# A planner's due times replaced by a written list of 1348 instructions: linear attention with a Hyena gate on one core

## The chip, the cores and the metric

The kernel runs on one core of a Trainium2 chip. The metric is the device time of one execution in microseconds (us); for a kernel it is the median over its runs. A profiled execution has an own time and a span, from its first to its last instruction; the span is a little shorter.

## The reference

Two layers follow each other. Batch is 8, heads 8, sequence S = 576, head width 64; 128 random features; model width 512.

```python
# attention with positive random features (per batch and head)
scale = 1 / sqrt(sqrt(64))
def phi(x):                                # x: q*scale or k*scale
    h = x @ omega.T - sum(x*x)/2
    return exp(h - max(h)) / sqrt(128)     # max over the features
kv  = phi(k).T @ v                         # 128 x 64
z   = sum over s of phi(k)
x   = (phi(q) @ kv) / (phi(q) @ z + 1e-6)  # 576 x 64; heads side by side: 576 x 512

# gated long convolution (per batch)
x1, x2, x3 = split(x @ w_proj, 3)          # 576 x 512 each
y   = x1 * irfft(rfft(x2) * rfft(filter)) * x3
out = y @ w_out
```

## The kernel before

**The attention.** The sequence of a batch is cut into a main part of 512 rows and a left part of 64, and the left parts of two batches are worked on as one tile of 128 rows. For each batch, keys are transposed (by TensorE through the one-bank PSUM tile "t", or from batch 5 on by a transposing DMA of SyncE), multiplied with omega into the two-bank tile "a2" (64 contraction rows), and put through ScalarE's exponential into ek (`key_features`). VectorE finds the largest feature of each row, whose reciprocal scales the values (`weigh_values`, giving vc). Queries go the same way into eqt. The sums kv come out of eight groups of matmuls; the rows of the output are divided by their denominators on VectorE (`normalise`) and turned back into xt. Loads are DMAs that GpSimd issues: k and v in one DMA of 512 KB for a batch, q from batch 2 on in four pieces of 128 KB, each left part in two halves of 64 KB. GpSimd issues in order, so a load whose buffer is not free stands ahead of all later loads.

**The convolution.** With S = 3 x 192, the transform is three transforms of length 192 over folded inputs, done as matmuls with tables of sines that the kernel makes at its start (`make_residues`, `sines`, `tables`). For each pair of batches: `fold` combines the three thirds of xt into xf, `project2` multiplies it by w_proj into x2, `forward` transforms and multiplies by the filter's spectrum, `gates` makes x1 * x3 (x13; of the left rows x13l), then come the inverse and the product with w_out. These use the PSUM tiles "h", one bank each, three of them in turn. The filter itself is folded and transformed once (`fold_filter`, `filter_transform`).

**What sets the order of issue.** The kernel's body isn't issued as it is written. `nc` is a `Plan`: every call on an engine is recorded as an `Op` with its number n, the tiles it reads and writes, and the stage and batch that `at` set; neighbouring matmuls into one tile are joined into one `Op`. 1348 are recorded: 396 of TensorE (PE), 475 of VectorE (DVE), 306 of ScalarE (ACT), 81 of GpSimd (POOL), 90 of SyncE (SP). Then `issue` emits them in the order that `order` returns. All instructions of the body so have line 405 in the profile, the line in `issue`; one tells them apart by the names of their tiles.

Before, `order` gives each operation a due time: the latest one at which its users could still be on time, worked back from the end of its batch (`PERIOD` and `STRETCH`), shifted by tables of numbers by stage, batch and engine (`LEAD`, `SHIFT`, `LEAN`). `simulate` then runs the program with modelled durations (`_cost`) and on each engine takes, of the operations that could start within 120 ns of the first, the one that is due first. It also hands out buffers in the order of its own program for each kind of tile and stage. The emitted instructions wait, as ever, for their data and for the buffer's earlier readers: a tile is given a slot of its pool when the first instruction that uses it is issued, so the order of issue also settles which earlier tile's readers a new tile waits for.

**The operations that are spoken of below**, by their number n:

| n | engine | what |
|---|---|---|
| 41 | DVE | factors for the residues (`make_residues`) |
| 224, 225 | PE, DVE | transposes of half of keys 2, and their copy into kt |
| 130, 131 | PE, ACT | turning back a quarter of the output rows of batch 0, and its copy into xt |
| 127 | PE | output rows of batch 0 (`a2` from kv and eqt) |
| 179 | ACT | last exponential of queries 1 |
| 600 | PE | first product of `fold` 0 (xf with w_proj, a bank h) |
| 248, 236 | PE | transposes of queries 2; of the left keys of batches 2 and 3 |
| 354, 417 | POOL | loads of keys 5, of keys 6 (512 KB each) |
| 145, 146 | POOL | two of the four pieces of queries 2 |
| 212 | POOL | one half of the left keys of batches 2 and 3 |
| 642 | SP | one of the moves of the filter's spectrum into hqs |
| 736, 435, 438 | DVE | the gate of the left rows, x13l, of the first pair; two steps of weighing values 5 |
| 823 | PE | a product of `fold` 3 (bank h) |
| 900, 949 | PE | a product of `gates` 3; one of the inverse of batch 3 |
| 809, 812 | DVE, PE | the fold of batch 2; the first product on it |
| 724, 697, 710, 828 | DVE | gate of batch 1, left spectrum, spectrum of batch 1, fold of left rows |
| 372 | PE | transposes of the left keys of batches 4 and 5 |
| 687, 267 | ACT | a copy of `forward` 0 (xs), the copy of kv of batch 2 |
| 367 | DVE | a copy of keys 4 into kt |

Of the kernel before, what the change touches and what calls it, by code (L numbers as in the profile page):

```python
# [24 lines left out]
PERIOD, STRETCH, STAY = 136.732, 16.038, 101.39  # L25
LEAD = {
    "cross keys": 0.92, "cross out": 7.64, "cross queries": -0.74, "filter": 4.65, "fold": -48.94,
    "forward": 107.85, "gates": -40.51, "inverse": 17.39, "keys": -0.75, "left keys": -52.95,
    "left out": -1.12, "left queries": -14.15, "load filter": 50.17, "load k": 55.36,
    "load kl": -1.11, "load q": -0.71, "load ql": 8.56, "load v": 0.49, "load vl": 1.73,  # L30
    "load w0": 1.61, "load w1": 5.28, "load w2": 1.64, "out": -42.88, "queries": 96.24,
    "residues": 1.41, "rest": 14.42, "sines": 0.5, "start": -189.65, "sums": -10.66,
    "tables": 0.2, "turn out": -3.18, "turn queries": 16.85, "values": -5.78, "zeros": 9.94,
}

SHIFT = {
    ("fold", 0): 48.94, ("fold", 1): 188.96, ("fold", 2): 50.05, ("fold", 7): 48.3,
    ("forward", 0): -112.16, ("forward", 1): -114.87, ("forward", 2): -107.32,
    ("forward", 6): -108.25, ("gates", 0): 16.24, ("gates", 1): 40.13, ("gates", 2): 50.94,
    ("gates", 6): 38.24, ("left keys", 2): 53.69, ("left keys", 6): 49.69, ("load k", 2): -56.64,  # L40
    ("load q", 0): -1.89, ("load ql", 0): -33.49, ("load v", 0): 2.07, ("load vl", 2): -6.7,
    ("queries", 1): -97.56, ("queries", 2): -131.03, ("queries", 6): -98.12,
    ("queries", 7): -93.75, ("rest", 1): 207.08, ("rest", 7): -14.42, ("turn out", 1): -12.03,
    ("turn out", 2): -153.32, ("turn queries", 1): -15.77, ("turn queries", 2): -16.64,
    ("values", 1): 546.29, ("values", 2): -24.51,
}
LEAN = {
    ("forward", "DVE"): 35.53, ("forward", "PE"): -40.96, ("gates", "DVE"): -10.03,
    ("gates", "PE"): 146.99, ("keys", "ACT"): -14.86, ("left queries", "ACT"): -47.8,
    ("queries", "ACT"): 5.49, ("queries", "PE"): 33.51, ("rest", "ACT"): -8.58,  # L50
    ("rest", "DVE"): -16.93,
}
# [33 lines left out]
class Op:  # L86
    __slots__ = (
        "eng", "calls", "reads", "writes", "due", "n", "busy", "lat", "deps", "users",
        "tiles", "start", "end", "name", "dma", "table", "where", "rows", "base",
    )  # L90

    def __init__(self, eng, due, n, name, where):
        self.eng, self.due, self.n, self.name, self.where = eng, due, n, name, where
        self.calls, self.reads, self.writes = [], [], []
        self.busy = self.lat = 0.0
        self.deps, self.users = {}, []
        self.tiles = set()
        self.dma = self.table = None
        self.rows = 128
# [13 lines left out]
class Plan:  # L113
# [4 lines left out]
    HOP = {"PE": 55.0, "DVE": 37.0, "ACT": 37.0, "POOL": 60.0, "SP": 60.0}  # L118

    def __init__(self, nc, tc):  # L120
        self.nc, self.tc = nc, tc
        self.ops, self.tile_of, self.slots = [], {}, {}
        self.where = "start", 0
        self.tensor = Proxy(self, "PE", nc.tensor)
        self.vector = Proxy(self, "DVE", nc.vector)
        self.scalar = Proxy(self, "ACT", nc.scalar)
        self.gpsimd = Proxy(self, "POOL", nc.gpsimd)
        self.sync = Proxy(self, "SP", nc.sync)
        self.allow_low_precision = nc.allow_low_precision
# [4 lines left out]
    def _new(self, eng, name):  # L134
        stage, b = self.where
        more = LEAD.get(stage, 0.0) + SHIFT.get((stage, b), 0.0) + LEAN.get((stage, eng), 0.0)
        op = Op(eng, more, len(self.ops), name, self.where)
        self.ops.append(op)
        return op

    def tile(self, pool, shape, dtype, name, bufs=1):
        t = pool.tile(shape, dtype, name=name, bufs=bufs)
        key = t.name if hasattr(t, "name") else t[:].tensor.name
        self.slots[pool.name, name] = bufs
        line = self.where[0]
        self.tile_of[key] = ((pool.name, name), "residues" if line == "load filter" else line)
        return t
# [7 lines left out]
    def record(self, eng, real, name, args, kw):  # L155
# [16 lines left out]
        if join:  # L172
            op = last
        else:
            op = self._new(eng, f"{name} {outs[0].tensor.name}")
            op.rows = ins[0].ap[0][1] if eng == "PE" else 128
# [5 lines left out]
        self._cost(op, eng, name, outs, ins)  # L182
        if name == "activation":
            op.table = {AF.Exp: "exp", AF.Sin: "sin"}.get(kw["func"])
        return op

    def opaque(self, eng, call, out, busy):
# [3 lines left out]
        op.busy = op.lat = busy  # L191

    @staticmethod
    def _free(ap):
        n = 1
        for _, c in ap.ap[1:]:
            n *= c
        return n

    def _cost(self, op, eng, name, outs, ins):  # L200
        out = outs[0]
        n = self._free(out)
        if name == "dma_start_transpose":
            op.busy, op.lat = 2000.0, 2200.0
            op.dma = ("HW", self._free(out) * 128 * 2 / 240.0)
            return
        if name == "dma_start":
            a = out if out.space != bass.MemoryType.DRAM else ins[0]
            run = a.ap[-1][1] * SIZE[a.dtype]
            rows = a.ap[0][1] * self._free(a) // a.ap[-1][1]  # L210
            if eng == "POOL":
                op.busy, op.lat = (880.0 if rows > 600 else 720.0), 3300.0
                op.dma = ("SW", rows * max(run, 166) / 198.0)
            elif out.space != bass.MemoryType.DRAM and ins[0].space == bass.MemoryType.DRAM:
                op.busy, op.lat = 580.0, 2300.0
                op.dma = ("HL", rows * run / 330.0)
            else:
                op.busy, op.lat = 580.0, 2000.0
                op.dma = ("HW", rows * run / 180.0 / (1 if out.space == bass.MemoryType.DRAM else 4))
            return  # L220
        half = all(SIZE[a.dtype] == 2 for a in (out, *ins))
        sbuf = all(a.space != bass.MemoryType.PSUM for a in (out, *ins))
        if eng == "PE":
            m = n / (4.8 if ins[0].ap[0][1] == 64 else 2.4) + 2.5
            op.lat = op.busy + n / 2.4 + 166.0
            op.busy += m
            return
        if eng == "DVE":
            if name == "memset":
                busy = n * SIZE[out.dtype] / 4.8 + 5.0  # L230
            elif name == "reciprocal":
                busy = 5.8 * n + 78.0
            elif name == "tensor_tensor":
                busy = n / (1.92 if half and sbuf else 0.96) + 68.0
            elif name == "scalar_tensor_tensor":
                busy = n / 0.96 + 130.0
            elif name in ("tensor_copy", "tensor_scalar", "tensor_scalar_mul"):
                rate = (4 if sbuf else 2) if half else (2 if sbuf else 1)
                if name != "tensor_copy" and not sbuf:
                    rate = 1  # L240
                busy = n / (0.96 * rate) + (68.0 if half else 100.0)
            elif name == "reduce_max":
                busy = self._free(ins[0]) / 0.96 + 60.0
            else:
                busy = n / 0.96 + 68.0
            op.busy, op.lat = busy, busy + 82.0
        elif eng == "ACT":
            busy = n * 0.8333 + (52.0 if not sbuf else 190.0)
            op.busy, op.lat = busy, busy + 107.0
        else:  # L250
            op.busy = op.lat = n / 1.2 + 100.0

    def order(self):
        last = {}
        for op in self.ops:
# [6 lines left out]
            for key, kind in ((op.reads, 0), (op.writes, 1)):  # L262
                for t, r in key:
                    last[t].append((op, kind, r))
                    if t in self.tile_of:
                        op.tiles.add(t)
        for op in self.ops:
            for o in op.deps.values():
                o.users.append(op)
        for op in reversed(self.ops):  # L270
            lat = op.lat + (op.dma[1] if op.dma else 0.0) + 50.0
            last = min((u.base for u in op.users), default=op.where[1] * PERIOD)
            op.base = last - STRETCH * lat / 1000.0
        for op in self.ops:
            op.due += op.base
            if op.eng == "PE":
                for u in op.users:
# [4 lines left out]
    def simulate(self):  # L282
# [8 lines left out]
        for op in ops:  # L291
            for t in op.tiles:
                left[t] = left.get(t, 0) + 1
# [1257 lines left out]
```

## Time and profile before

| | |
|---|---|
| runs | 266.75, 267.43, 267.69 us; median 267.43 |
| profiled execution, own time | 266.88 us |
| its span | 264.8 us |
| TensorE clock granted | 1.00 of full speed throughout |
| busy: PE, DVE, ACT, POOL | 239.7, 213.4, 195.2, 61.3 us |
| DMA | 36.31 MB, mean 137 GB/s |

Busy time is the time in which an engine had an instruction under way; loads of TensorE's weights (PEld) overlap its matmuls. "Idle before" is the time between the end of one instruction and the start of the next on the same engine, and the releaser is what the trace shows as ended last before it. An idle stretch of an engine costs something only where the end of the program hangs on that engine.

### The profile page before, as it was taken

How to read it: one execution, taken by the hardware profiler on the slowest of the kernel's cores; microseconds unless marked ns; L12 is line 12 of the kernel's file. 1: busy time of each engine (PE TensorE's matmuls, PEld its weight loads, DVE VectorE, ACT ScalarE, POOL GpSimd, SP SyncE). 2: the span in 40 equal slices, each digit the busy share in tenths (PEclk: the TensorE clock that was granted, in tenths of full speed). 3: DMA queues.
4: the chain of work that ended last, by engine and by line, in shares of the span. 5: the costliest groups of instructions: out<-in, count | busy, mean ns of one | idle time of the engine just before them, and what ended most of it. 6: DMA issues, size and time to landing. Idle time of an engine off the chain costs nothing. (4 is left out here: it accounts for less than half of the span.)

```text
span 264.8 us, 5724 instructions
## 1 busy us (share of the span) xinstructions
PE 239.7 (91%) x2202; PEld 135.3 (51%) x2234; DVE 213.4 (81%) x475; ACT 195.2 (74%) x307; POOL 61.3 (23%) x86
## 2 busy tenths in 40 slices
PE   0576689999999999989999999999999999999994
PEld 0444445565476547546456454447455554446541
DVE  7999975689959999998499995979989788188470
ACT  6699499759999988986938976997495565753523
POOL 8634474444831610650040000000000000000000
PEclk9999999999999999999999999999999999999999
DMA  7999999999997978899679169524316311430406
GB/s 178 195 198 189 202 204 200 204 168 188 185 156 132 110 114 159 87 157 189 195 92 177 44 141 220 119 108 135 74 35 182 90 42 38 149 71 2 157 1 198
DMA packets 88866, 36.31 MB, mean 137 GB/s; under 512 B 60299, under 2 KB 83336, under 8 KB 88840
## 3 DMA queue, kind: packets, MB, share of 16 engines
q0 software_dynamic: 58560, 16.78, 61.4%
q1 hardware_dynamic: 30136, 19.04, 29.6%
q8 instruction: 17, 0.28, 0.4%
q10 hardware_dynamic: 144, 0.13, 0.1%
q14 instruction: 9, 0.07, 0.1%
HBM read 34.64 MB, written 9.44 MB: 166 GB/s over the span
## 5 line engine op out<-in xcount | busy, mean ns | idle before, releaser
L405 ACT CAST x<-h 128x512 bf16<-128x512 f32 x68 | 39.8, 596 | 31.5 <-PE h L405 28.4
L405 PE MATMUL h<-xt,wproj 128*128 128x512 bf16 x240 | 59.4, 380 | 1.3 <-DVE bt L405 0.4
L405 PEld LDWEIGHTS <-wproj 128*128 128x128 bf16 x384 | 31.2, 98 | 27.6 <-issue 2.7
L405 ACT ACTIVATE eqt<-a 128x1024 bf16<-128x1024 f32 x32 | 32.2, 1065 | 4.6 <-PE a L405 4.6
L405 ACT ACTIVATE osb<-h 128x512 f32<-128x512 f32 (+4 forms) x49 | 28.2, 575 | 7.3 <-PE h L405 5.9
L405 ACT ACTIVATE ek<-a 128x1024 bf16<-128x1024 f32 x32 | 32.1, 1046 | 0.5 <-PE a L405 0.2
L405 PE MATMUL h<-wproj,xf 128*128 128x512 bf16 x120 | 30.5, 379 | 1.7 <-DVE x13l L405 0.7
L405 PE MATMUL h<-wout,yt 128*128 128x512 bf16 x127 | 30.9, 379 | 0.4 <-DVE yt L405 0.3
L405 POOL DMA_DIRECT2D qn<-in_q_dram x26 | 22.9, 893 | 33.5 <-DMA qt<-qn 19.0
L405 DVE TENSOR_TENSOR x<-h,x 128x512 bf16<-128x512 f32 x32 | 21.8, 684 | 6.4 <-PE h L405 5.6
L405 DVE TENSOR_TENSOR bt<-h,osb 128x384 f16<-128x384 f32 x32 | 16.5, 552 | 7.8 <-PE h L405 5.3
L405 PEld LDWEIGHTS <-yt 128*128 128x128 bf16 x128 | 11.9, 98 | 14.8 <-issue 0.9
L405 PEld LDWEIGHTS <-xf 128*128 128x128 bf16 x134 | 12.2, 98 | 13.9 <-issue 1.5
L405 PE MATMUL h<-x,fwb 128*128 128x512 bf16 x68 | 18.3, 379 | 0.4
L405 PE MATMUL h<-gtab,xs 128*128 128x384 bf16 x64 | 15.6, 326 | 0.0
L405 PE MATMUL a<-om,kt 64*128 64x128 bf16 x256 | 11.5, 218 | 2.9 <-DVE kt L405 1.4
L405 PEld LDWEIGHTS <-eqt 128*128 128x128 bf16 x256 | 10.9, 98 | 5.7 <-DVE xb L405 1.3
L405 DVE TENSOR_TENSOR xb<-a,rden 128x512 bf16<-128x512 f32 x20 | 13.3, 684 | 0.4
L405 PE MATMUL a<-kv,eqt 128*128 128x65 bf16 x256 | 12.0, 194 | 1.0 <-DVE xb L405 1.0
L405 PE MATMUL a<-qt,om 64*128 64x512 bf16 x64 | 11.4, 383 | 0.9 <-ACT eqt L405 0.3
L405 PEld LDWEIGHTS <-kt 64*128 64x128 bf16 x256 | 7.5, 94 | 8.8 <-issue 5.5
L405 DVE TENSOR_TENSOR xf<-xt 128x1024 bf16<-128x1024 bf16 (+1 forms) x16 | 8.6, 551 | 4.2 <-ACT xt L405 4.2
(159 smaller groups left out, 471.2 us busy)
## 6 DMA issues: line engine op xcount, KB each, us to landing
out_dram<-osb SPq DMA_DIRECT2D x24, 256.0 KB, 2.3
vn<-in_v_dram POOLq DMA_DIRECT2D x8, 512.0 KB, 9.6
kn<-in_k_dram POOLq DMA_DIRECT2D x7, 512.0 KB, 8.4
qn<-in_q_dram POOLq DMA_DIRECT2D x24, 128.0 KB, 7.4
sw<-sp SPq DMA_DIRECT2D x16, 128.0 KB, 2.3
wproj<-in_moe_w_proj_dram POOLq DMA_DIRECT2D x3, 512.0 KB, 10.1
ek<-in_k_dram SPq DMA_DIRECT2D x2, 512.0 KB
qn<-in_q_dram POOLq DMA_DIRECT2D x2, 512.0 KB, 10.1
```

The source lines that it names most:

```text
L405: getattr(real, name)(*args, **kw)
```

## The change

`order` no longer plans. A string `ORDER` holds the 1348 numbers in the order of issue over all engines; `order` works out which operation needs which (as before), reads the list, and asserts that no operation stands ahead of its data. Due times, the modelled costs and `simulate` are gone, and with them the planner's own account of buffers; a tile gets its slot when its first instruction is issued, as before. The body of the kernel, its tiles, its pools and its operations are the same. The first operation of ScalarE is the same, a sine (n = 29) on one column.

```diff
-PERIOD, STRETCH, STAY = 136.732, 16.038, 101.39
-LEAD = {
-    "cross keys": 0.92, "cross out": 7.64, "cross queries": -0.74, "filter": 4.65, "fold": -48.94,
...
-}
-SHIFT = {
...
-LEAN = {
...
-}
+ORDER = """
+    0 57 30 31 32 7 1 6 37 5 39 9 28 140 2 33 29 58 12 40 8 34 41 13 24 46 38 17 25 42 27 47 43 44
...
+    112 81 151 114 103 152 156 592 104 154 153 96 157 155 105 158 182 160 106 159 107 161 221 113
+    183 97 166 116 115 162 167 117 20 184 163 118 185 149 119 164 186 120 121 165 124 122 125 224
+    123 18 126 127 128 172 129 174 622 173 595 625 225 147 175 176 626 130 216 218 178 177 624 131
+    636 168 627 179 169 132 226 133 628 623 170 637 629 213 171 228 643 134 638 180 644 641 135
+    646 651 645 649 181 136 227 137 187 653 631 597 630 230 229 188 632 600 354 148 189 634 654
+    598 599 190 214 193 601 191 604 194 192 219 602 231 605 195 650 196 215 603 606 647 197 652
+    198 633 217 233 608 232 199 85 235 610 223 212 200 607 220 639 234 201 609 611 202 252 612 614
+    203 613 640 648 635 616 615 146 253 204 207 254 145 205 208 618 617 206 665 209 290 620 717
...
+    663 352 320 267 348 687 690 263 286 321 691 366 265 324 367 674 325 693 326 268 302 661 269
...
+    697 725 710 478 365 828 809 346 355 347 698 812 727 827 699 370 369 711 814 423 813 713 737
...
+    1338 1339 1343 1341 1342 1344 1345 1347 1346
+"""
...
     def tile(self, pool, shape, dtype, name, bufs=1):
-        t = pool.tile(shape, dtype, name=name, bufs=bufs)
...
-        return t
+        return pool.tile(shape, dtype, name=name, bufs=bufs)
...
-        self._cost(op, eng, name, outs, ins)
...
-        return self.simulate()
-
-    def simulate(self):
...
-    WINDOW, SPAN = 120.0, 3413.0
+        order = [self.ops[int(n)] for n in ORDER.split()]
+        place = {op.n: i for i, op in enumerate(order)}
+        assert len(place) == len(order) == len(self.ops)
+        for op in order:
+            assert all(place[n] < place[op.n] for n in op.deps), "an instruction before its data"
+        return order
```

Where some of the operations stand on their engine (place, counted from 0, and the operation just ahead on that engine):

| n | engine | before | after |
|---|---|---|---|
| 41 | DVE | 8, behind 40 | 12, behind 34 |
| 224 | PE | 32, behind 127 | 31, ahead of 127 |
| 225 | DVE | 82, behind 129 | 84, behind 625 |
| 131 | ACT | 32, behind 179 | 31, behind 178 |
| 687 | ACT | 76, behind 260 | 82, behind 267 |
| 809 | DVE | 166, behind 711 | 168, behind 828 |
| 372 | PE | 127, behind 812 | 135, behind 753 |
| 736 | DVE | 228, behind 830 | 223, behind 383 |
| 900 | PE | 233, behind 949 | 232, behind 943 |
| 642 | SP | 6 | 17 |
| 354 | POOL | 47 | 33, behind 213 |
| 212 | POOL | 28 | 41, behind 223 |
| 146, 145 | POOL | 32, 31 | 43, 44 |
| 417 | POOL | 59 | 61 |

Of the slots: keys 5 (354) follow keys 2 in their buffer instead of keys 3; keys 6 follow keys 5 instead of keys 4; queries 2 and queries 3 take each other's buffer. The bank of 823 was the one that 736 reads last, and is another; the banks of 600 and of 900 also follow other tiles.

## Prediction

> **What bounds the kernel now.** I read the page first: shares of the engines, then the 40 slices of TensorE (6.6 us each).
>
> ```profile
> span 264.8 us, 5724 instructions
> PE 239.7 (91%) x2202; PEld 135.3 (51%) x2234; DVE 213.4 (81%) x475; ACT 195.2 (74%) x307; POOL 61.3 (23%) x86
> ...
> PE   0576689999999999989999999999999999999994
> ```
>
> TensorE (PE) is busy 91% of the span and its zeros, fives and sixes all lie in the first seven slices. Since the change only re-orders, what matters is where PE is idle; so I cut the span by stages (columns: stretch, length, then busy time of PE, PEld, DVE, ACT, POOL; granted clock; DMA share; GB/s).
>
> ```profile
> 0.00:10.00 10.00, 0.90 (x5) 0.58 (x6) 8.01 (x34) 6.37 (x10) 9.26 (x20) 1.00 1.02 183
> 10.00:20.00 10.00, 8.12 (x101) 5.94 (x100) 9.45 (x29) 8.80 (x11) 3.29 (x5) 1.00 1.46 198
> 20.00:30.00 10.00, 6.64 (x128) 5.00 (x128) 9.72 (x19) 7.67 (x10) 4.28 (x7) 1.00 1.50 195
> 30.00:43.30 13.30, 10.44 (x125) 6.76 (x128) 8.95 (x19) 10.88 (x17) 8.59 (x11) 1.00 1.38 201
> 43.30:116.00 72.70, 71.17 (x768) 42.43 (x780) 64.19 (x133) 64.16 (x98) 31.46 (x40) 1.00 1.41 155
> 116.00:261.00 145.00, 142.44 (x1076) 74.60 (x1093) 112.79 (x247) 96.94 (x163) 4.39 (x5) 1.00 0.55 110
> ```
>
> From 10 to 30 us VectorE (DVE) is busy 19.2 of 20 us and sets the pace; from 30 to 43.3 ScalarE (ACT) does most; from 43.3 PE has only 1.5 us idle in 72.7, then 2.6 us in 145, the latter partly the tail of single products. So the ceiling of a new order is small behind 43.3 us, and 17 us of idle in front of it is held by other engines' work, of which the order can save little unless it also shortens their chains. Three idle stretches of PE are the ones that I found touched (timeline; in brackets the idle time before, and the releaser):
>
> ```profile
> 30.70 0.43 PE L405 MATMUL a<-kv,eqt 128*128 128x65 bf16 x8 [1.00 <-DVE xb L405]
> ...
> 43.26 1.02 PE L405 MATMUL h<-wproj,xf 128*128 128x512 bf16 x4 [0.51 <-ACT osb L405]
> ...
> 116.62 1.89 PE L405 MATMUL h<-wproj,xf 128*128 128x512 bf16 x8 [0.69 <-DVE x13l L405]
> ...
> 150.08 1.02 PE L405 MATMUL h<-xt,wproj 128*128 128x512 bf16 x4 [0.42 <-DVE bt L405]
> ```
>
> [...]a step between matmuls of 64 and of 128 rows costs 95 to 98 ns more than one within a kind (median, both directions). [...]The trace goes further for GpSimd's (POOL's) loads: each lands after the one issued before it, 512 KB about 2.7 us and a 128 KB piece of the queries about 0.9 us after its predecessor.
>
> **The change part by part.** [...]The order changes on PE for 137 of 396, by at most 8 places; on DVE for 351 of 475 (up to 27 places), ACT 117 of 306, POOL 72 of 81, SP 57 of 90; and as buffers are given out when an operation is issued, 207 of 822 tiles follow another tile in their slot. Numbers below are those of the list.
>
> *0 to 30 us.* DVE clears two buffers (memsets 0.50 and 0.91 us in the trace) in another order, the factors of the residues (41) come about 0.5 us later, the exponentials' table load by 0 to 0.3. DVE bounds from there, with the same operations by the 60th. Value loads and filter pieces move on POOL, but queries 0 and 1 need 14.7 and 26.3 us, and by cumulative KB would land at 12.8 and 24: hidden. I take **+0.1** (0 to +0.3).
>
> *30 to 43 us.* The transposes of keys 2 (224) are put into PE's 1.00 us wait, so what follows it on PE is earlier and ACT's first exponential of queries 1 starts 0.2 to 0.5 earlier. ACT then runs from 32.01 to 43.2 with one gap:
>
> ```profile
> 32.01 3.77 ACT L405 ACTIVATE eqt<-a 128x1024 bf16<-128x1024 f32 x4 [3.65 <-PE a L405]
> ...
> 38.46 0.58 ACT L405 CAST xt<-t 128x512 bf16<-128x512 f32 x1 [0.27 <-PE t L405]
> ...
> 41.98 1.23 ACT L405 ACTIVATE osb<-h 128x512 bf16<-128x512 f32 x2
> ```
>
> The last line is what PE waits for at 43.26: it frees the bank of 600. The copy 131 is now ahead of 179, which makes the transposes that share one bank earlier and closes the 0.27. So 0.2 + 0.27 = 0.47 earlier, nearly the whole 0.51: **-0.5** (0 to -2.0, if more of the 2.9 us that PE idles here goes with it). What pays: DVE copies keys 225 behind three filter operations, 0.7 us later at PE 130, which lies ahead of ACT's need.
>
> *116.62.* The bank of 823 was that freed by 736, the multiply that ends at 116.57:
>
> ```profile
> 115.89 0.68 DVE L405 TENSOR_TENSOR x13l<-h,x 128x512 bf16<-128x512 f32 x1
> ```
>
> In the list 823 follows another tile in that slot, and 736 goes ahead of 435 on DVE. **-0.69** (0 if the next bank is as late). The price is that the values of batch 5 (438) come about 1.1 us later, 115.5 against a need at 119.6.
>
> *150.08.* 900 goes ahead of 949 and into a bank that is free earlier: **-0.42** (0 to -0.42).
>
> *Row changes.* Of 64 and 128 rows on PE: 70 after 43 us become 72, 2 x 97 ns = **+0.2**. In front of 43 there are two more, inside waits.
>
> *75 and 86 us.* DVE's fold 809 goes behind 724, 697, 710, 828:
>
> ```profile
> 85.46 1.02 DVE L405 TENSOR_TENSOR xf<-xt 128x1024 bf16<-128x1024 bf16 x2
> ...
> 86.58 1.03 PE L405 MATMUL h<-wproj,xf 128*128 128x512 bf16 x4
> ```
>
> The matmul started 0.10 after the fold. By the durations of what is put before it, the fold ends at 87.0, so PE waits up to 0.5; 372 is also moved. I take **+0.3** (0 to +0.55). ACT's 687 behind 267 delays DVE's 367 by about 0.6 at 76 us: **+0.1** (0 to +0.3). All behind it on DVE is late by the same, and hidden.
>
> *Loads.* POOL is a queue in order. Load 354 (keys 5, 512 KB) goes from place 47 to place 33 and takes the buffer of keys 2, last read at 42.58; so POOL stands from about 33.5 until then, with two loads still under way (576 KB, some 3 us). Behind it are one half of the left keys (212) and two pieces of queries 2 (146, 145, places 43 and 44 instead of 32 and 31). PE needs them here:
>
> ```profile
> 61.86 0.40 PE L405 MATMUL t<-ident,kl 128*128 128x128 bf16 x4
> ...
> 63.38 0.62 PE L405 MATMUL t<-ident,qn 128*128 128x128 bf16 x8
> ```
>
> Before, they landed at 42.6 and 48.1. Against the first 45 loads of before, the new 45 have 354 in place of one 128 KB piece: 2.7 - 0.9 = 1.8 us. The 45th landed at 62.00, so 145 lands at 63.8 when the pace stays; adding the shortest spacings seen gives 59 to 62. Margin -0.4 to +4: I take **0**, and hold the other end as a rival. Later keys 6, queries 5 and 6 are 3 us or more ahead of need, also with 417 waiting for the transpose at 91.5. SP's moved stores have no reader in the kernel, and a moved filter piece (642) lands at about 75 for 81.6.
>
> Sum: +0.1 - 0.5 - 0.69 - 0.42 + 0.2 + 0.3 + 0.1 = **-0.9 us**. The profiled execution took 266.88 us (264.8 span, 2.1 around it), so 266.0; it lies 0.55 below the median of 267.43. I give the median: 267.4 - 0.9 = **266.5**.
>
> **The rivals.**
>
> *Slower: the load queue.* One mechanism: 145 lands after PE reaches 248, which by the sum above is at about 62.9 (63.4 less the 0.5 of the stage before). For: the same-pace estimate of 63.8, and POOL standing 9 us in front. Against: the shorter spacings. It decides from a landing at 63.8, where the wait of 0.9 equals the whole gain. If the transfers also run dry while POOL stands until 42.6 (3 us of work under way, a fresh load landing some 3.4 us after its issue at the quickest: 0.5 to 1.5 us lost), 145 lands at 64.3 to 65.3, PE waits 1.4 to 2.4, and does nothing else meanwhile, so it all goes on the end: 266.5 + 1.4 to 2.4 = **267.9 to 268.9**, likeliest 268.5.
>
> *Nothing: what is won is eaten.* The waits of 0.69 and 0.42 pass to the next bank (1.1 back, 267.6), or 76 and 86 us cost their upper bounds (0.45 back, 267.0), or 145 lands just at 63.8 (267.4): **267.3**. It is also the case in which the order only moves hidden work.
>
> *More.* PE is near 100% only where nothing waits; if most of the idle in 31 to 43 goes (2.0 rather than 0.5), 266.5 - 1.5 = **265.0**. For it: the 1.00 wait is filled with 0.61 us of work; against: ACT's chain there, which PE can't pass.
>
> **How the numbers follow.** The forecast of small gains has 0.45, the larger gain 0.13, nothing 0.18, the load queue 0.24. 0.3%, about what a measurement of this kernel can tell from no change, is 0.8 us: faster is below 266.6, slower above 268.2. The forecast lies on that edge: I give 0.32 of its 0.45 to faster, as the chains of the first 43 us can give more than I took; with the larger gain, 0.45. Of the load queue 0.20 lies above 268.2, and 0.06 of the rest with it, for what my list of waits doesn't hold: 0.26. Same: 0.29. The range reaches from the larger gain to the dry load queue, and 0.3 over it for the first stage's upper bound: 264.9 to 269.2.
>
> **What would show it.** Right: no idle before the matmuls now at 43.26, 116.62 and 150.08, ACT without a gap from about 31.6 to 42.8, a wait of about 0.3 at a matmul of x and wproj near 86. Wrong: a wait of PE on a load of queries or left keys near 62, a first exponential over 0.5 us later, or PE's busy time itself changed by more than 0.3. If the end moves by over 1 us with none of these, my list of touched waits is incomplete.

## The result, and the profile after

The kernel with the written list takes **270.33 us** (median of 4 runs, 269.37 to 272.11) against 267.32 (4 runs, 266.75 to 267.69): ratio 1.0119, 95% interval 1.009 to 1.0148. It is slower by 3.0 us, where 0.9 less was forecast, and lies above the top of the range (269.2). The profiled execution took 270.55 us, with a span of 268.8. The medians and ranges below leave out two slow runs, one of e11 (278.33) and one of e13 (272.35).

First the page (busy time of the engines; PE and its granted clock in 40 slices of 6.7 us):

```profile
span 268.8 us, 5728 instructions
...
PE 245.4 (91%) x2234; PEld 137.6 (51%) x2234; DVE 212.7 (79%) x475; ACT 195.0 (73%) x307; POOL 61.9 (23%) x86
...
PE   0677799997999999999999979999999999999994
...
PEclk9998879999999999999999999999999999999998
```

Two things stand out. PE is *busier* by 5.7 us although the operations are the same, and the clock, which was full in the profile of before, falls to 7 and 8 tenths in the fourth to sixth slice. The matmuls on the slower clock show a longer busy time: three of `yt` with `fwb` take 1.31 us at 35.04 in the new kernel (a mean clock of 0.57 from there to 36.36), and 0.85 at 36.70 before, at 1.00. (PE's busy time was also a little too low before: 2202 of 2234 matmuls are in that record.) The stages that were bound by DVE and ACT, as shown before (PE, PEld, DVE, ACT, POOL busy; clock; DMA share; GB/s):

```profile
20.00:30.00 10.00, 8.00 (x128) 6.13 (x129) 8.85 (x15) 7.50 (x10) 4.05 (x6) 0.83 1.36 202
30.00:43.30 13.30, 11.32 (x118) 6.61 (x118) 8.81 (x21) 10.20 (x15) 3.14 (x4) 0.87 1.49 195
```

DVE, which set the pace with 9.72 us of work from 20 to 30, does 8.85 now, beside a PE on a clock of 0.83. The bracketed waits of PE that answer to those of before, from its timeline:

```profile
44.07 1.02 PE L232 MATMUL h<-wproj,xf 128*128 128x512 bf16 x4
...
62.97 0.38 PE L232 MATMUL t<-ident,kl 128*128 128x128 bf16 x4 [0.62 <-DMA kl<-in_k_dram]
...
65.42 0.62 PE L232 MATMUL t<-ident,qn 128*128 128x128 bf16 x8 [0.88 <-DMA qn<-in_q_dram]
...
88.75 1.04 PE L232 MATMUL h<-wproj,xf 128*128 128x512 bf16 x4 [0.25 <-DVE xf L232]
...
115.62 0.24 PE L232 MATMUL h<-gta,sp 128*128 128x192 bf16 x1 [0.37 <-DVE x13l L232]
...
116.82 1.03 PE L232 MATMUL h<-wproj,xf 128*128 128x512 bf16 x4
...
156.47 1.90 PE L232 MATMUL h<-wproj,xf 128*128 128x512 bf16 x8 [1.41 <-DVE xf L232]
...
159.15 0.43 PE L232 MATMUL a<-kv,eqt 128*128 128x65 bf16 x8 [0.52 <-DVE h L232]
```

The waits that the prediction wanted gone (0.51 ahead of 600, now at 44.07; 0.69 ahead of 823; 0.42 at 150) are gone. New ones stand at the loads near 63 and 65 and at the fold of batch 4 (991, at 156.47). To find where the time went I compared PE's operation at the same place of its order in both traces (new less before, us, by the start of its first weight load; in the first row, where that load ran far ahead, by its first matmul):

| us in the trace before | new less before | what lies between |
|---|---|---|
| 25.0 | -0.48 | the new head is ahead |
| 29.3 | +0.30 | clock 0.50 from 24.99 to 28.41 in the new kernel |
| 40.8 | +1.61 | clock 0.50 from 35.23 to 38.65 |
| 46.3 | +0.65 | the 0.51 and other waits are gone |
| 56.4 | +0.42 | |
| 66.6 | +1.85 | waits of 0.62 and 0.88 for loads |
| 89.7 | +2.48 | fold 2 |
| 119.2 | +1.71 | the 0.69 is gone |
| 147.5 | +2.20 | |
| 157.1 | +3.94 | waits of 1.41 and 0.52 at fold 4 |
| 254.8 | +4.04 | |

Both kernels do not always get the same clock: 52 further runs of the kernel before had a mean clock of 0.9925, and took 267.04 us on average in the ten runs at 1.00, 267.69 in the sixteen at 0.994 and 269.10 in the seven at 0.984. Where that matters below, times are given at like clocks.

### The profile page after: what moved, and what is told of

Read it like the earlier page. It is cut to its first block, busy times and chain, and to the rows that moved or that the text cites. A ratio compares the mean times of both kernels' runs of the same rounds, so it can differ in the third digit from the quotient of the medians.

```text
span 268.8 us, 5728 instructions
## 1 busy us (share of the span) xinstructions
PE 245.4 (91%) x2234; PEld 137.6 (51%) x2234; DVE 212.7 (79%) x475; ACT 195.0 (73%) x307; POOL 61.9 (23%) x86
## 5 line engine op out<-in xcount | busy, mean ns | idle before, releaser
L232 PE MATMUL h<-xt,wproj 128*128 128x512 bf16 x256 | 61.5, 380 | 0.0
L232 ACT ACTIVATE osb<-h 128x512 f32<-128x512 f32 (+4 forms) x49 | 27.3, 565 | 9.2 <-PE h L232 7.4
L232 PE MATMUL h<-wproj,xf 128*128 128x512 bf16 x128 | 31.4, 379 | 1.9 <-DVE xf L232 1.7
L232 PE MATMUL h<-x,fwb 128*128 128x512 bf16 x72 | 19.0, 379 | 0.0
L232 PE MATMUL a<-kv,eqt 128*128 128x65 bf16 x256 | 12.7, 196 | 0.9 <-DVE h L232 0.5
## 6 DMA issues: line engine op xcount, KB each, us to landing
qn<-in_q_dram POOLq DMA_DIRECT2D x24, 128.0 KB, 8.0
sw<-sp SPq DMA_DIRECT2D x16, 128.0 KB, 2.3
```

The lines of the kernel that those rows point to most:

```text
L232: getattr(real, name)(*args, **kw)
```

## The experiments

Theory L: the new order of GpSimd's loads costs the time, near 63 and near 156. Theory C: the half clock does. Theory M: fold 4 is late since its matmul 410 was moved 5.6 us later on PE.

All experiments write another list; e9, e10, e12 and e13 also add twelve matmuls to the body, and the others keep it. "new" and "before" are an engine's operations in the two orders. Beside each kernel the one before was run, with medians of 267.51 to 267.61.

**e1: GpSimd as before.**

```diff
-GpSimd = new
+GpSimd = before
```

> The new list, with GpSimd's 81 operations put back into the order of before (and with them the buffers of keys, queries and filter pieces); PE, DVE, ACT and SP keep the new order. Theory L (the loads): PE's waits on loads at 62.97 (0.62) and 65.42 (0.88) go, and the fold of batch 4 (988) is no longer late, since the load of values 7 no longer runs beside the transposing DMA 416 (6.4 us of issue and 12.8 us to landing in the new kernel, 4.3 and 7.1 before): -1.3 and -1.4 to -2.2, so 267.0 to 267.6 against 270.3. Theory C (the half clock of 25.0 to 28.4 and 35.2 to 38.6 is what costs): nothing changes there, 269.5 to 270.3. Theory M (416 is late because its matmul 410 was moved 5.6 us later on PE): the wait of 1.4 at 991 stays, 269.

Measured: 268.96 (17 runs, 268.43 to 270.34). The waits near 63 and 65 and at 991 are gone, so theory M falls: 410 still stands where the new list has it. But a new wait appears in the head. PE's and DVE's timelines of this kernel:

```profile
24.55 0.40 PE L230 MATMUL a<-om,kt 64*128 64x128 bf16 x8 [3.19 <-DVE kt L230]
```
```profile
23.48 0.42 DVE L230 TENSOR_TENSOR vcl<-vl,vcl 64x512 bf16<-64x512 bf16 x1 [2.32 <-DMA vl<-in_v_dram]
```

The new DVE order scales the left values ahead of a copy of keys, and so needs their load earlier; the two orders belong together. Behind this, e1 gains 2.27 us on the new kernel on the way from 150 to 164: its PE goes from 0.63 late to 1.64 early against it.

**e2: only GpSimd in the new order.**

```diff
-GpSimd = before
+GpSimd = new
```

> The kernel before, with only GpSimd's operations in the new order. Theory L: +1.3 near 62 to 66 and up to +2.2 near 153, so 269.5 to 271 against 267.3, a slowdown as large as the whole change's. Theories C and M: 267.3 to 268.6, the waits on loads alone.

Measured: 275.48 (4 runs, 274.96 to 275.81), ratio 1.0277 (1.0223 to 1.033): +8, beyond every theory. PE waits 0.44 for queries 2 and 6.93 at 949. Why, e11 shows.

**e3 and e4: the head alone.**

```diff
-PE, DVE, ACT, SP = new
+PE, DVE, ACT, SP = before[:57]+new[57:], before[:104]+new[104:], before[:50]+new[50:], before[:18]+new[18:]
```

> The new list, with the first 46 us of PE, DVE, ACT and SP in the order of before (PE's first 57 operations, DVE's 104, ACT's 50, SP's 18); GpSimd keeps the new order. Theory C: no half clock, and 1 to 1.6 us less, 268.7 to 269.3. Theory L: the new head gave nothing and cost 0.4 at 46 us, so 269.9 to 270.3.

> The kernel before, with only the first 46 us of PE, DVE, ACT and SP in the new order; GpSimd as before. Theory C: two spells of half clock of 3.4 us as in the new kernel and 268.3 to 268.9 against 267.3. Theory L: 267.3 to 267.8, the half clock paid for by waits that were there before.

(e4 is the same cut the other way round: the head in the new order, the rest and GpSimd as before.) Measured: e3 269.80 (20 runs), e4 269.19 (20 runs). e3 had a mean clock of 0.992, that of the kernel before, and is still 2.2 us slower than it: so the clock is not the main part. e4 is inconclusive, as it has the wait of e1 in its head (2.97 us).

**e5: the late loads as before, the early ones as in the new list.**

```diff
-GpSimd = new
+GpSimd = new[:25] + before[25:]
```

> The new list; GpSimd keeps its first 25 operations, which the new head of DVE needs (values of the left rows ahead), and from there on takes the order of before. Theory L (loads): PE's waits on loads at 63.0 and 65.4 go (-1.4) and the fold of batch 4 is on time (-2.3): 266.4 to 267.2 against 270.3; the half clock of the first 40 us stays. Theory C (half clock): 269.5 to 270.

Measured: **267.02** (20 runs, 265.94 to 267.94), ratio to before 0.9974 (0.9959 to 0.999). With one queue's order changed from its 26th operation on, 3.3 us come back. No wait of PE for a load is left near 63 and 65, nor one at 991. That is theory L, in size and place.

**e6: two loads moved.**

```diff
-GpSimd = ... 475 480 482 477 479 481 483 419
+GpSimd = ... 475 477 483 480 482 479 481 419
```

> The new list with two loads moved: values 7 (483, 512 KB) and a half of their left rows (477) go ahead of the four pieces of queries 7, as they stood before; buffers as in the new list. Theory L in its narrow form: they then land by about 131, no longer beside the transposing DMA 416, which lands 6 to 7 us after its issue and not 12.8; PE's waits at 991 (1.41) and 463 (0.52) go: 268.0 to 268.5. If it were the pieces of queries 7 alone, or the matmul 410 that was moved 5.6 us later, nothing changes: 270.3.

Measured: 267.16 (12 runs, 266.53 to 268.31), less than was expected. That is 3.2 less than the new kernel; at like clocks, of which there are few runs, 2.2 (267.14 at 0.991, against 269.37) to 2.8 (267.78 at 0.987, against 270.55 at 0.985). (Its profiled execution had the full clock throughout, which that of the new kernel had not.) The waits near 62 and 64 stay (1.18 and 0.60), that at 991 is gone. 483 now lands at 128.0 instead of 152.3, and the transposing DMA 416, issued at 141.24, lands at 148.89. On SP's queue, before (first) and in the new kernel (second), it stands as

```profile
139.96 4.30 SPq L405 DMA_TRANSPOSE xt<-h  x1
```
```profile
142.89 6.36 SPq L232 DMA_TRANSPOSE xt<-h  x1
```

and lands, by the trace, at 147.07 before and 155.69 in the new kernel: 7.1 and 12.8 us after its issue. It carries the output rows of batch 4; DVE's fold waits for it:

```profile
155.72 1.03 DVE L232 TENSOR_TENSOR xf<-xt 128x1024 bf16<-128x1024 bf16 x2 [2.17 <-DMA xt<-h]
```

In e6 the matmuls of this fold follow their predecessor without a wait:

```profile
153.26 1.67 PE L230 MATMUL h<-wproj,xf 128*128 128x512 bf16 x7
```

**e7: one load moved.**

```diff
-GpSimd = ... 213 354 148 214 ... 284 222 287 289 351 ...
+GpSimd = ... 213 148 214 ... 284 222 287 289 354 351 ...
```

> The new list with one load moved: keys 5 (354) go behind 289 as before, and keys 4 and 5 get the buffers of before. Theory L: GpSimd doesn't stand from 35.6 to 44.3, left keys and queries 2 land 5 us or more earlier, PE's waits at 63.0 and 65.4 (0.62 + 0.88) go, the rest stays: 268.7 to 269.1. If the transfers and not the standing set it: one of the waits stays, 269.5 to 270.3.

Measured: 270.60 (4 runs, 269.69 to 272.15). In the profile the waits near 63 and 65 are gone, and PE ends 0.9 earlier than in the new kernel; the median doesn't show it, as the clocks of these few runs were lower (mean 0.983 against 0.986). Inconclusive by itself; e13 repeats it.

**e8: the tail alone.**

```diff
-PE, DVE, ACT, SP = before
+PE, DVE, ACT, SP = before[:57]+new[57:], before[:104]+new[104:], before[:50]+new[50:], before[:18]+new[18:]
```

> The kernel before, with PE, DVE, ACT and SP in the new order only from 46 us on (their first 57, 104, 50 and 18 operations as before), GpSimd as before. The prediction's terms behind 46 us, alone: -0.69 at 116.6, -0.42 at 150, +0.2 for two more row changes, +0.3 at 86 and +0.1 at 76: -0.5 against before, 266.8 to 267.2. Rival: other new waits of DVE and ACT (0.37 at 759, 0.33 at 1044 in the new kernel) eat it: 267.3 to 267.8.

Measured: 267.07 (20 runs) against 267.53, ratio 0.9984 (0.9966 to 1.0003); at full clock 266.46 (6 runs) against 266.87 (9), at 0.994 267.14 (4) against 267.61 (17). All three say -0.4 to -0.5, which the sum of those terms had, though the interval of the ratio just includes no change.

**e9 and e10: PE kept busy in the head.**

```diff
+    def busy_work(ps):        # in e9 on the list of e5, in e10 on that of before
+        nc.tensor.matmul(out=ps[:, 0, :], lhsT=ident[:],
+                         rhs=gtab[:].rearrange("p m c -> p (m c)")[:, 0:512],
+                         start=True, stop=True)
...
             ps = two_banks()
             made.append(ps)
+            if nc.where == ("keys", 1):
+                busy_work(ps)
...
                         ps = two_banks()
                         made.append((pr, ps))
+                        if b < 2:
+                            busy_work(ps)
```

> The kernel of e5 (new list, late loads as before) with twelve idle matmuls added on PE in the first 36 us: one of 512 columns and 128 rows on a table of sines, overwritten by the real product, ahead of each tile of keys 1, queries 0 and queries 1 (0.22 us each, 2.6 in all). Theory C (PE is put on half clock after a 3.41 us stretch with too little work, and that took the head's gain): no half clock in most runs, 265.9 to 266.4 against 267.0 for e5. Rival: the half clock doesn't depend on what PE does there, or PE's added work delays the exponentials: 267.0 to 268.

> The kernel before with the same twelve matmuls. Theory C: 266.7 to 267.1, as its runs at full clock (266.9), without the ones at 269. Rival: 267.5 and more.

Measured: e9 **265.18** (6 runs, 264.98 to 265.82), ratio to before 0.9924 (0.9899 to 0.9948), all six at a clock of 0.998 or more. Twelve useless matmuls take 1.8 us off e5, and this beats both kernels. (One run of e5 had the full clock by itself, and took 265.96; so about 1.1 of the 1.8 is the clock as far as one run can tell, and what the rest is stays open.) e10: 267.74 (20 runs), no gain; its clock rose only to a mean of 0.9967, and its runs at full clock took 267.56, 0.4 more than those of before beside it (267.16). The theory holds for most of the gain on the new head, and the rival (the added work is in the way) for the old.

What the half clock (0.50) follows is seen when the new kernel is cut at the clock's own steps:

```profile
21.58:24.99 3.41, 1.89 (x37) 1.36 (x38) 3.28 (x6) 3.33 (x5) 1.01 (x2) 1.00 1.40 199
24.99:28.41 3.42, 3.42 (x50) 2.79 (x47) 2.60 (x3) 1.88 (x3) 1.62 (x3) 0.50 1.34 202
...
31.82:35.23 3.41, 1.99 (x13) 0.82 (x12) 3.35 (x9) 3.14 (x4) 1.94 (x3) 1.00 1.52 189
35.23:38.65 3.42, 3.42 (x18) 1.65 (x17) 3.20 (x6) 2.53 (x5) 0.32 (x1) 0.50 1.40 199
```

Each of these two stretches of 3.41 us at half clock comes after one of the same length in which PE was busy for under 2.0 us (1.89 and 1.99); in e5 the two before were 1.65 and 1.84. In e1 and e4 two such stretches follow each other: ahead of the first PE was busy for 0.76 and 0.45 us, ahead of the second for 2.82 and 2.90, but at half clock. In e9 the least is 2.54 us in such a stretch, and none is halved:

```profile
29.01:32.43 3.42, 2.54 (x25) 1.22 (x22) 3.34 (x10) 0.93 (x2) 0.68 (x1) 1.00 1.25 204
```

In the new kernel and in e5 PE was not idle ahead of them: it was busy for about half of the stretch (1.65 to 1.99 of 3.41 us). Why executions of one kernel differ in their clock (0.984 to 1.00 for the kernel before) isn't shown.

**e11: the two loads of e6, moved in the kernel before.**

```diff
-GpSimd = ... 476 477 474 475 483 479 480 481 482
+GpSimd = ... 476 474 475 479 480 481 482 477 483
```

> The kernel before with two loads moved: values 7 (483) and a half of their left rows (477) go behind the four pieces of queries 7; all else, buffers too, as before. Theory L, narrow: the transposing DMA 416 lands 10 to 14 us after its issue instead of 7.1, ScalarE waits for the store of an osb tile that is queued behind it on SP, and PE stands at 949: +4 to +8.5, 271.5 to 276. If the +8 of e2 came from other loads (the last piece of queries 6 among them): 267.5 to 269.

Measured: **274.35** (3 runs, 272.72 to 274.96), ratio 1.025 (1.0206 to 1.0294). One load of 512 KB and one of 64 KB, issued 24 and 26 us later and still far ahead of their need, cost 7 us. SP, ACT and PE of this kernel:

```profile
140.62 4.84 SPq L230 DMA_TRANSPOSE xt<-h  x1
145.55 1.20 SPq L230 DMA_DIRECT2D out_dram<-osb  x2
```
```profile
154.99 0.48 ACT L230 CAST osb<-h 128x384 f16<-128x384 f32 x1 [6.48 <-DMA out_dram<-osb]
```
```profile
155.91 0.32 PE L230 MATMUL h<-gta,sp 128*128 128x192 bf16 x1 [6.04 <-ACT osb L230]
```

The transposing DMA lands at 153.95, 13.3 us after its issue, and values 7 at 155.12, 14.6 after theirs. Two stores are issued behind the transpose, at 145.55 and 146.15; ACT waits until 154.99, 1.04 us after the transpose landed, for one of their osb buffers (in the kernel before, the median store lands 2.3 us after its issue), and PE waits 6.04 for ACT. Stores held up behind the transpose would fit ACT's wait; the trace has no landing of these two, so it isn't shown. In the new list no store is issued behind 416 on SP until 156.55, 0.86 us after it landed, and there only the fold is late: the same two loads cost 2 to 3 us there and 7 here.

**e12 and e13: the new kernel and e7, each with the twelve matmuls of e9.**

> The whole new list, GpSimd's order too, with the twelve idle matmuls of e9: the clock is taken out of the sum. What is left over e9 (265.2) is the loads alone, both places: +2.3 at 156 and +0.5 to +1.4 at 62 to 66, so 268.0 to 268.9 at full clock; the clock term of the change itself is then 270.3 less that, 1.4 to 2.3. Rival: the loads' waits were made by the half clock, which held GpSimd's buffer until 43.8: without it queries 2 are in time and 267.5 is seen.

> As e12, with keys 5 (354) behind 289 again and the buffers of keys 4 and 5 as before (e7 without the clock's noise). Theory L: less than e12 by the waits of 62 to 66, 0.5 to 1.4: 267.2 to 268.0, and +2.3 over e9 at 156. Rival: the same as e12, and the loads of 62 to 66 cost nothing in the end.

Measured: e12 269.29 (8 runs, 268.66 to 270.94), e13 268.41 (19 runs, 266.74 to 269.67), both above what was expected. So, in medians: clock 270.33 - 269.29 = 1.0; loads near 62 to 66, e12 less e13, 0.9; the other late loads, those beside the transposing DMA among them, e13 less e9, 3.2. In e12 PE waits 0.94 and 0.64 near 62 with the clock full there (a mean of 0.997 in that profile), so these waits weren't made by the half clock:

```profile
61.25 0.38 PE L232 MATMUL t<-ident,kl 128*128 128x128 bf16 x4 [0.94 <-DMA kl<-in_k_dram]
...
63.46 0.62 PE L232 MATMUL t<-ident,qn 128*128 128x128 bf16 x8 [0.64 <-DMA qn<-in_q_dram]
...
155.24 1.04 PE L232 MATMUL h<-wproj,xf 128*128 128x512 bf16 x4 [2.13 <-DVE xf L232]
```

A part of the 3.2 is again the clock: in e13's profile the wait of 2.17 at 991 is itself followed by 3.41 us at half clock, and that of 2.13 in e12's isn't. PE reached 991 about 1 us earlier than in e12, and both end within 0.1 us of each other in their profiles.

## Why the prediction was wrong, point by point

**The step that failed** is the sentence on loads: "Later keys 6, queries 5 and 6 are 3 us or more ahead of need", and values 7 were not named at all: the sum had nothing for them. Each load was judged by when its own data are used, and values 7, used at 179, could wait. What it runs beside was never asked. GpSimd's stop for queries 7, which was there before (19.0 us in its waits), now (17.43 us, until 138.16) holds values 7 behind it, and releases them, issued at 142.30, into the transposing DMA of batch 4, issued at 142.89: 2.3 us at that place in the traces of e1, 2.2 to 2.8 by e6, 7 in the kernel before (e11). (The half load of left values was moved with them in e6 and e11, and the two weren't tried apart.) Even the need was misjudged: the last piece of queries 6 lands at 154.53, and its transpose, issued at 151.46 before, goes out at 154.71.

**The rival of the load queue was right in mechanism and place, but its price was less.** It had 145 landing at 64.3 to 65.3 and PE waiting 1.4 to 2.4, all of it on the end; it landed at 65.38, and PE waited 0.62 for the left keys and 0.88 for the queries. That the landing fits is luck: at full clock (e12) it was 63.42. The forecast's own value, 0, was the term that failed here. GpSimd's stand is plain:

```profile
34.86 0.69 POOL L232 DMA_DIRECT2D kl<-in_k_dram  x1
44.26 0.88 POOL L232 DMA_DIRECT2D kn<-in_k_dram  x1 [8.71 <-PE t L232]
```

It ended 1.7 us later than the 42.6 of the prediction, as the half clock had put off the transposes that free the buffer (they end at 43.96). But e12, with 42.17, still had both waits: there PE comes 2.0 us earlier too, at 60.31 instead of 62.35 for the left keys. The median price, 0.9 us (e12 less e13), is over half of e12's waits.

**The head** (+0.1 and -0.5): the waits went as described, and the size was too small. At full clock the operation that PE had reached at 46.34 comes at 44.94 (e12) or, without added matmuls, at 45.05 (e6's profile): 1.3 to 1.4 earlier, toward the prediction's other end of 2.0. In the new kernel it comes at 46.99: the half clock costs 2.05 there, and 1.0 at the end. The failed step here is that the clock, 1.00 before, got no term, though the list moves PE's work in stretches where it idles a third of the time (6.64 of 10 us busy from 20 to 30 before). ACT without a gap was not seen in the new kernel, where it idles 0.89 at 37.25, but is in e12. That PE's busy time changed, here by 5.7 us, was one of the signs of being wrong that the prediction had named.

**The tail** (-0.69, -0.42, +0.2, +0.3, +0.1 = -0.5) was right in its sum, as e8 measured -0.46, but in part by luck. The waits of 0.69 and 0.42 are gone in e8's profile too; the 0.69 passed on in part (0.37 ahead of 759, for the same x13l), the wait at 812 was 0.25 where 0.3 was taken, and one of 0.33 at 1044 was not in the prediction. So 0.95 of new waits stands against 1.11, and of the 0.28 by which this profile's span is shorter, some 0.2 is there before 46 us, where the lists are the same. Where the rest of the 0.46 comes from isn't shown.

Together, from 267.5 for before: -0.46 for the tail (e8), nothing more from the head on the clocks that it got (e5 is at 267.02, e8 at 267.07), and 3.3 for the late loads (270.33 - 267.02).

## What to carry to other kernels

When loads are moved in a queue that stands at a buffer, list what each released burst will run beside, transposing DMAs above all (416 landed 12.8 us after its issue here, and 7.1 before), and what is queued behind those; slack to a load's own use said nothing on that. When work of a TensorE that idles a third of the time is moved, count its busy time in stretches of 3.41 us, the length of the half clocks here: useless matmuls paid in e9 (265.18 against 267.02 in e5), though in e10 they did not (267.74 against 267.51). And judge one engine's order with the order of the queue that feeds it: the new head needed the early loads in the new order (e1), and the rest ran better with the late loads in the old one (e5).

## What was not expected of the hardware

- The transposing DMA 416 took 5.5 to 7.9 us to land where four or five pieces of 128 KB were issued close ahead of it (eight kernels), and 12.6 to 13.9 where values 7, 512 KB, were issued within a microsecond of it, and the 64 KB of left values up to 3 us ahead, as well (seven kernels). Values 7 took 14.6 and 15.3 us in e11 and e2, 10.9 before. Which of the two holds the other was not tried.
- Half clock was also seen with one late operation: with the wait of 6.04 us at 949 in e11 the trace shows 6.83 us of it, and behind that of 2.17 at 991 in e13 3.41.
- How little work goes ahead of a half clock isn't settled: 1.99 us busy in 3.41 was followed by it, and 1.94 (e8), 2.00 (before) and even 1.76 (e12, at its wait of 2.13 near 154) were not. So the busy time of such a stretch alone doesn't tell it.
